# Loads of x in an FFT-mixing and feed-forward kernel: eight single steps or four pairs

## The chip, the cores and the metric

The kernel runs on one core of one Trainium2 chip. Its time is the device time of one execution in microseconds (us). Times of the kernel before are the median of three runs; a profile is one further execution with the hardware profiler.

## The reference

Eight sequences of 3008 positions by 256 channels are filtered in the frequency domain along the positions, and the result goes through a feed-forward layer with a PReLU-like step:

```python
X = np.fft.rfft(x, axis=1)                      # x: (8, 3008, 256)
Y = X * (filt_r + 1j * filt_i)[None, :, :]
y = np.fft.irfft(Y, n=3008, axis=1)             # then (24064, 256)
h = y @ w_in                                    # (256, 2048)
g = np.maximum(h, 0.0) + alpha * np.minimum(h, 0.0)
out = g @ w_out                                 # (2048, 256)
```

Everything that is multiplied is in 16-bit floating point; inputs and the output in HBM are 32-bit.

## The kernel before

**Two works in one stream.** The feed-forward layer is cut into 48 blocks of 512 (sometimes 384) rows of y. Each block has 16 steps `j`, so there are 768 steps, and the main loop at the end of the kernel (from line 690) runs over them. In a step it issues, in this order: what was held back (`flush`), the `sums` of a block that are due, whatever `plan` holds for the step, the held-back additions (`settle`), the two matmuls of `up(j)` (line 498), and then so many matmuls of an earlier block's second product as keep that about 17 steps behind (`LAG`).

**The FFT of the next batches is threaded through this by a plan written by hand.** `put(step, fn, ...)` appends a call to a step's list; calls of one step run in the order in which they were put. A batch covers six blocks, so its period is 96 steps, and for batch `b` the plan counts from `p = 96 * (b - 1)`. The stages of a batch are

- `load_x` (line 170): x of the batch goes from HBM to the tile `xs`, cast to 16 bits. A batch has four chunks `c` (0 to 3), each with two halves `h` of 47 partitions; one half is one transfer of 188 KB, issued on GpSimd's queue (POOL). `xs` has four buffers.
- `piece_a` (line 211): one matmul on `xs`; ScalarE evicts it to `asb`. Sixteen pieces, four for each chunk. `save_a` and `turn_a` move the result through HBM into `at`, on SyncE's queue (SP).
- `piece_b` (line 231): two matmuls on `at`; VectorE makes `ww` and `uu` (lines 234, 235), and two accumulating transfers on POOL's queue add `ww` into `uu` with halves swapped (line 237).
- `piece_c` (line 249): two matmuls on `uu`. `turn_c` (line 258) stores the result and `load_z` (line 267) loads it back as `zt`, both on SP's queue.
- `piece_d` (line 274): matmuls on `zt` that give `yT`, which the blocks read.

**Fast blocks.** Every second block from block 8 on (`FAST`) does its second product with seven half-size products in place of eight (`seven`, line 559). For that, sums of pieces of `gtb` are made beforehand (`sums`): some on VectorE, and some as accumulating transfers on POOL's queue (line 524), `gtb<-gtb` and, last, `gtb<-ss`. The last of the seven products reads what `gtb<-ss` wrote. In steps of a batch's period, the transfers of line 524 are due at steps 10, 17 and 20 of each pair of blocks, so at -22, -15, -12, 10, 17 and 20 around a period's start.

**The lines around the change.** `STEPS_Q` (line 39) holds the steps, counted from `p` of batch `b`, at which the eight halves of x of batch `b + 1` are loaded, for `b` of 3 to 6, that is, for batches four to seven; chunk `c`, half `h` uses entry `2 * c + h`:

```python
for h in range(2):
    put(p + STEPS_Q[2 * c + h], load_x, b + 1, c, (h,))
```

These are put ahead of the same batch's `piece_b`, so at an equal step the load comes first. The first `piece_a` of batch `b + 1` stands at step 12 of that count (`STEPS_A[0]` is -84 of the next period), those of the later chunks begin at steps 31, 40 and 46. The `piece_b` of batch `b` stand at `STEPS_B` (-21, -15, 4, 6, 13, 21, ...), and for `b = 3` at -11, -9, 0, 5, 10, 18, ...; `piece_c` of the third and fourth of them at 16 and 19 (`b = 3`: 16 and 22).

An engine's instructions run in the order in which they are issued, each waiting for what it needs; POOL's and SP's queues do so too.

Of the kernel before, what the change touches and what calls it, by code (L numbers as in the profile page):

```python
# [35 lines left out]
STEPS_F = (20, 16, 22, 28, 34)  # L36
STEPS_K = (118, 121, 128, 133, 144)
STEPS_X = ((20, 27, 42, 52), (107, 109, 113, 126))
STEPS_Q = (-28, -18, -8, -3, 1, 9, 15, 23)
FIRST = (  # L40
# [61 lines left out]
def kernel(  # L102
# [514 lines left out]
    def put(step, fn, *args):  # L617
        plan.setdefault(step, []).append((fn, args))
# [17 lines left out]
    for b in range(1, NB):  # L636
# [7 lines left out]
        if b + 1 < NB:  # L644
            for c in range(4):
                if b < 3:
                    put(STEPS_X[b - 1][c], load_x, b + 1, c)
                else:
                    for h in range(2):
                        put(p + STEPS_Q[2 * c + h], load_x, b + 1, c, (h,))  # L650
        quarters, later = (4, 1) if b < 3 else (1, 4)
# [97 lines left out]
```

## Time and profile before

| | us |
|---|---|
| median of 3 runs | 778.01 (777.71 to 780.72) |
| the profiled execution | 778.49 |
| its span | 776.7 |
| TensorE (PE) busy | 759.6 (98%) |
| VectorE (DVE) busy | 691.0 (89%) |
| ScalarE (ACT) busy | 606.1 (78%) |
| GpSimd (POOL) busy | 264.7 (34%) |

The granted TensorE clock was 0.997 over the span. "PEld" in the rows is the load of weights, which overlaps PE. A row of the timeline gives start, duration, engine, line, operation, tiles out<-in, how many were merged, and in brackets the idle time ahead with what ended it. A row of waits gives who waited for whom: total us, how often, longest. A row of windows gives the stretch, its length, each engine's busy time with its count, the PE clock, the share of the 16 DMA engines' time that was in use (overlaps can take it above 1) and GB/s. "DMA to landing" is the time from the start of an issue to the landing of its data.

### The profile page before, as it was taken

How to read it: one execution, taken by the hardware profiler on the slowest of the kernel's cores; microseconds unless marked ns; L12 is line 12 of the kernel's file. 1: busy time of each engine (PE TensorE's matmuls, PEld its weight loads, DVE VectorE, ACT ScalarE, POOL GpSimd, SP SyncE). 2: the span in 40 equal slices, each digit the busy share in tenths (PEclk: the TensorE clock that was granted, in tenths of full speed). 3: DMA queues.
4: the chain of work that ended last, by engine and by line, in shares of the span. 5: the costliest groups of instructions: out<-in, count | busy, mean ns of one | idle time of the engine just before them, and what ended most of it. 6: DMA issues, size and time to landing. Idle time of an engine off the chain costs nothing.

```text
span 776.7 us, 18287 instructions
## 1 busy us (share of the span) xinstructions
PE 759.6 (98%) x6952; PEld 541.9 (70%) x6952; DVE 691.0 (89%) x1517; ACT 606.1 (78%) x902; POOL 264.7 (34%) x351
## 2 busy tenths in 40 slices
PE   7899999999999999999999999999999999999998
PEld 6756667666676767766677767767677777777776
DVE  3788996799999999999899999989999999989994
ACT  4687678888788887888878888788878777787773
POOL 6830641144234342353233422434222333103210
PEclk9999999999999999999999999999999999999999
DMA  9996858666997679886797869966786645635642
GB/s 181 191 191 185 163 110 209 185 130 138 192 201 153 125 162 189 207 151 129 162 196 151 156 136 178 210 134 131 161 191 153 127 86 103 167 84 105 129 96 68
DMA packets 112879, 118.74 MB, mean 153 GB/s; under 512 B 12616, under 2 KB 94296, under 8 KB 112792
## 3 DMA queue, kind: packets, MB, share of 16 engines
q0 software_dynamic: 32656, 47.99, 38.4%
q1 hardware_dynamic: 79992, 69.52, 33.7%
q8 instruction: 54, 0.88, 0.5%
q14 instruction: 33, 0.27, 0.1%
q10 hardware_dynamic: 144, 0.07, 0.0%
HBM read 56.06 MB, written 46.66 MB: 132 GB/s over the span
## 4 chain that ended last, share of the span: by engine, by line
PE 87%; DVE 4%; DMA 4%; ACT 3%; issue 1%; POOL 1%; SPq 1%; DVEq 0%; ACTq 0%; POOLq 0%
PE hps L498 38%; PE op L537 20%; PE op L559 16%; PE psF L211 3%; PE psF L274 3%; PE psF L249 2%; PE psF L231 2%; ACT gtb L506 2%; DMA twf_s<-c_twf 1%; DVE m L509 1%; DVE gtb L685 1%; DMA zt<-v_dram 1%; PE op L592 1%; DVE ww L234 1%; DVE uu L235 1%
## 5 line engine op out<-in xcount | busy, mean ns | idle before, releaser
L506 ACT ACTIVATE gtb<-hps 128x1024 f16<-128x1024 f32 (+1 forms) x384 | 385.9, 1005 | 110.5 <-PE hps L498 106.5
L498 PE MATMUL hps<-yT,win_s 128*128 128x512 f16 (+1 forms) x1536 | 449.2, 374 | 0.0
L509 DVE TENSOR_SCALAR m<-gtb,alm_s 128x512 f16<-128x512 f16 (+1 forms) x768 | 235.1, 348 | 45.4 <-ACT gtb L506 43.7
L685 DVE TENSOR_TENSOR gtb<-gtb,m 128x1024 f16<-128x1024 f16 (+1 forms) x384 | 260.9, 679 | 14.2
L537 PE MATMUL op<-wout_s,gtb 128*128 128x256 f16 x1600 | 243.1, 272 | 0.0
L237 POOL DMA_DIRECT2D uu<-ww x168 | 142.2, 1014 | 263.1 <-DVE uu L235 165.2
L537 PEld LDWEIGHTS <-gtb 128*128 128x128 f16 x1600 | 156.0, 98 | 104.6
L498 PEld LDWEIGHTS <-win_s 128*128 128x128 f16 x1536 | 136.7, 98 | 25.6 <-issue 2.5
L559 PEld LDWEIGHTS <-gtb 128*128 128x128 f16 x1680 | 114.3, 98 | 53.8 <-DMA gtb<-ss 1.0
L524 POOL DMA_DIRECT2D gtb<-gtb x42 | 40.5, 963 | 192.9 <-DVE ss L518 62.1
L559 PE MATMUL op<-wout_s,gtb 128*128 128x128 f16 x1008 | 85.1, 219 | 1.1 <-ACT gtb L506 0.6
L281 ACT ACTIVATE asb<-psF 96x512 f16<-96x512 f32 x112 | 65.1, 594 | 9.7 <-PE psF L211 8.4
L281 ACT ACTIVATE yT<-psF 128x376 f16<-128x376 f32 x120 | 56.2, 486 | 10.5 <-PE psF L274 9.3
L559 PEld LDWEIGHTS <-ss 128*128 128x128 f16 x672 | 47.1, 98 | 23.3
L170 POOL DMA_DIRECT2D xs<-in_x_dram x64 | 54.4, 1014 | 14.2 <-PE psF L211 13.4
L559 PE MATMUL op<-tw_s,gtb 128*128 128x128 f16 x672 | 58.1, 219 | 0.0
L559 PE MATMUL op<-tw_s,ss 128*128 128x128 f16 x672 | 58.0, 219 | 0.0
L234 DVE TENSOR_TENSOR ww<-psF,filts_s 128x512 f16<-128x512 f32 x84 | 57.4, 684 | 0.3 <-PE psF L231 0.2
L235 DVE TENSOR_TENSOR uu<-psF,filt_s 128x512 f16<-128x512 f32 x84 | 57.2, 681 | 0.0
L281 ACT ACTIVATE v<-psF 128x512 f16<-128x512 f32 x84 | 49.0, 598 | 7.8 <-PE psF L249 7.2
L211 PE MATMUL psF<-xs,wf_s 94*96 94x512 f16 x112 | 41.2, 380 | 1.4 <-ACT yT L281 0.4
L274 PE MATMUL psF<-wi_s,zt 96*128 96x94 f16 x504 | 39.4, 205 | 2.2 <-ACT yT L281 1.4
(86 smaller groups left out, 524.9 us busy)
## 6 DMA issues: line engine op xcount, KB each, us to landing
out_dram<-osb SPq DMA_DIRECT2D x127, 128.0 KB
xs<-in_x_dram POOLq DMA_DIRECT2D x64, 188.0 KB, 5.8
a_dram<-asb SPq DMA_DIRECT2D x28, 384.0 KB
uu<-ww POOLq DMA_DIRECT2D x168, 64.0 KB, 3.0
v_dram<-v SPq DMA_DIRECT2D x112, 96.0 KB
zt<-v_dram SPq DMA_DIRECT2D x28, 384.0 KB
gtb<-gtb POOLq DMA_DIRECT2D x42, 256.0 KB, 4.5
at<-a_dram SPq DMA_DIRECT2D x20, 384.0 KB
```

The source lines that it names most:

```text
L211: nc.tensor.matmul(ps[0:96], wf1_s, xs[:, o : o + 512], start=True, stop=True)
L234: nc.vector.tensor_mul(ww, px, filts_s[:, 2 * kp : 2 * kp + 2])
L235: nc.vector.tensor_mul(uu, px, filt_s[:, 2 * kp : 2 * kp + 2])
L237: nc.gpsimd.dma_start(out=uu[o : o + 64], in_=ww[64 - o : 128 - o], accum_op=OP.add)
L274: nc.tensor.matmul(ps[:, m], self.zt[g][:, 4 * mh + m, dh * 128 : dh * 128 + 128], wi3_s, start=True, stop=True)
L281: nc.scalar.activation(o, i, AF.Copy)
L498: nc.tensor.matmul(self.hps[:, j % 2, 0:tn], win_s[:, kt, j * 128 : (j + 1) * 128], yT[:, kt, self.t0 : self.t0 + tn], start=(kt == 0), st ...
L506: nc.scalar.activation(g, hs, AF.Copy)
L509: nc.vector.tensor_scalar(ms[:, i], g[:, i], 0.0, a, OP.min, OP.mult)
L537: nc.tensor.matmul(op[:, si % 2], self.pair(k // 2)[:, k % 2, 128 * si : 128 * si + 128], wout_s[:, k], start=(k == 0), stop=(k == 15))
L559: nc.tensor.matmul(acc[:, 128 * i : 128 * i + 128], x[:, k, 128 * i : 128 * i + 128], b[:, k], start=first and k + i == 0, stop=k == 7, sk ...
L685: nc.vector.tensor_add(g, g, ms)
```

## The change

The eight steps of `STEPS_Q` become four equal pairs. Chunk 0 is loaded at -8 (both halves), chunk 1 at -4, chunk 2 at 0, chunk 3 at 4. Batches one to three are loaded as before.

```diff
-STEPS_Q = (-28, -18, -8, -3, 1, 9, 15, 23)
+STEPS_Q = (-8, -8, -4, -4, 0, 0, 4, 4)
```

## Prediction

> **What bounds the kernel now.** I read the page first: busy shares, the chain that ended last, the queues.
>
> ```profile
> span 776.7 us, 18287 instructions
> PE 759.6 (98%) x6952; PEld 541.9 (70%) x6952; DVE 691.0 (89%) x1517; ACT 606.1 (78%) x902; POOL 264.7 (34%) x351
> PE 87%; DVE 4%; DMA 4%; ACT 3%; issue 1%; POOL 1%; SPq 1%; DVEq 0%; ACTq 0%; POOLq 0%
> q0 software_dynamic: 32656, 47.99, 38.4%
> ```
>
> TensorE (PE) is busy for 98% of the span and is 87% of the chain. q0 holds the transfers that GpSimd (POOL) issues, the loads of x among them. The next view is busy time by windows, one window of 91 us for about each period of 96 steps in which the moved loads lie (us, then PE, PEld, DVE, ACT, POOL busy with counts, PE clock, DMA share, GB/s).
>
> ```profile
> 200.00:291.00 91.00, 90.72 (x825) 63.78 (x824) 84.31 (x185) 74.50 (x111) 33.66 (x42) 1.00 0.80 164
> 291.00:382.00 91.00, 90.15 (x839) 64.02 (x837) 85.33 (x191) 74.64 (x113) 32.87 (x43) 1.00 0.79 164
> 382.00:473.00 91.00, 91.00 (x831) 64.17 (x830) 84.75 (x186) 74.93 (x113) 31.14 (x41) 1.00 0.79 164
> 473.00:564.00 91.00, 90.09 (x835) 63.94 (x834) 84.89 (x191) 74.51 (x114) 32.94 (x43) 1.00 0.78 164
> ```
>
> PE's idle time in the four periods is 0.28 + 0.85 + 0.00 + 0.91 = 2.04 us. The change adds and removes no matmul, so 2.04 us is about all it can win; what it can lose has no such bound. So the question is which late transfer makes PE wait, and I asked for the waits in the last of the four periods and for the chain there.
>
> ```profile
> PE psF L274 <- DMA zt<-v_dram: 0.3, 1, 0.3
> PEld L559 <- DMA gtb<-ss: 0.8, 1, 0.8
> ```
> ```profile
> 490.32 3.22 DMA v_dram<-v
> 493.68 6.09 DMA zt<-v_dram
> ```
> ```profile
> 499.81 0.51 PE L274 MATMUL psF<-wi_s,zt 96*128 96x94 f16 x8 [0.28 <-DMA zt<-v_dram]
> 506.70 0.28 PE L559 MATMUL op<-wout_s,gtb 128*128 128x128 f16 x2 [0.62 <-ACT gtb L506]
> ```
>
> Two transfers arrive just too late: the first zt tile (0.28 us of idle PE) and gtb<-ss, the accumulate that the last product of a fast block reads (the weight load waited 0.8 us for it, PE idled 0.62 us; the matmul row names ACT, but the weight load in front of it names the DMA). 0.28 + 0.62 is that period's 0.91.
>
> **What the change moves.** POOL's timeline for that period (p = 480, the loads of batch seven):
>
> ```profile
> 475.12 1.21 POOL L170 DMA_DIRECT2D xs<-in_x_dram  x1
> 491.10 1.65 POOL L237 DMA_DIRECT2D uu<-ww  x2 [1.32 <-DVE uu L235]
> 492.16 1.14 POOL L170 DMA_DIRECT2D xs<-in_x_dram  x1
> 496.53 0.97 POOL L524 DMA_DIRECT2D gtb<-gtb  x1 [3.23 <-PE op L559]
> 500.01 1.51 POOL L524 DMA_DIRECT2D gtb<-ss  x1
> 500.59 2.54 POOL L170 DMA_DIRECT2D xs<-in_x_dram  x3
> 513.42 1.74 POOL L237 DMA_DIRECT2D uu<-ww  x2 [10.28 <-DVE uu L235]
> 515.74 1.74 POOL L237 DMA_DIRECT2D uu<-ww  x2 [0.58 <-DVE uu L235]
> 516.93 1.10 POOL L170 DMA_DIRECT2D xs<-in_x_dram  x1
> ```
>
> POOL works its list in order and does not follow PE's steps: it runs ahead until something makes it wait. The loads of steps -8, -3 and 1 already go out together at 500.59, right behind gtb<-ss (step -12), because nothing stands between them. All eight steps of the new list lie between that gtb<-ss and the uu of step 4 (the loads of step 4 are planned ahead of that uu). So the eight will go out as one burst from 500.59, not as four pairs; 475.12 (-28), 492.16 (-18), 516.93 (9) and the two after it (15, 23) go. In the period of batch three the uu steps are other (-11, -9, 0, 5), so there six go out, then a uu, then two.
>
> **Cost on POOL.** Nothing is added: the same eight issues. POOL idled 10.28 us before 513.42. Three issues began within one row of 2.54 us, so eight need at most 8 x 1.2 = 9.6 us (the longest single issue above is 1.21) and end by 510.2, ahead of 513.42. If that cover were gone, each extra microsecond would hold up the uu.
>
> There is one wait that the burst may bring: POOL waits for its own old transfers when many are out. At the start, where it issues loads in a row, it shows
>
> ```profile
> POOL filt_s L178 <- DMA xs<-in_x_dram: 1.6, 3, 0.7
> ```
>
> filt_s has nothing to do with xs, so these are waits for a free slot; the queue's semaphores come round. I take it that eight can be out. Then the loads behind the fourth wait until gtb<-gtb (496.53), the uu and gtb<-ss have landed, and the last load goes out when gtb<-ss lands, about 506.7. What queues behind it is the uu of 513.42, which by then needs only the first loads to have landed. Cost 0 while that is before 513.42.
>
> **Cost on the DMA engines.** Here is the real price.
>
> ```profile
> DMA to landing us min/median/max: 8.1/8.6/8.7
> DMA to landing us min/median/max: 4.0/4.0/4.0
> DMA to landing us min/median/max: 2.4/2.7/3.3
> ```
> ```profile
> 500.00:505.00 5.00, 5.00 (x76) 4.20 (x74) 4.67 (x14) 4.71 (x10) 3.13 (x5) 1.00 1.13 252
> 505.00:510.00 5.00, 4.38 (x50) 3.11 (x48) 3.25 (x9) 3.69 (x8) 0.00 (x0) 1.00 0.92 212
> 510.00:515.00 5.00, 4.99 (x40) 3.36 (x39) 4.94 (x11) 3.79 (x6) 1.58 (x2) 1.00 0.33 87
> 515.00:520.00 5.00, 5.00 (x39) 3.34 (x37) 4.86 (x12) 4.54 (x8) 3.33 (x5) 1.00 0.61 80
> 520.00:525.00 5.00, 5.00 (x41) 3.32 (x40) 4.93 (x11) 4.65 (x8) 2.22 (x3) 1.00 0.82 167
> ```
>
> The first three rows are times from issue to landing: the three loads sent together, the lone load of 516.93, the six uu from 513.42 on. How long does one load occupy the engines? From q0's row, 0.384 x 776.7 us for 47.99 MB is 6.2 us per MB; a load of 188 KB (0.193 MB) is then 1.2 us. The bounds: 0.193 MB at the 252 GB/s of the first window, 0.76 us; and the lone load's 4.0 us. The upper one can't be a rate, since three loads sent within about 1 us landed within 0.6 us of each other, so I take 1.2 us.
>
> The burst has five loads more than the three: 6.0 us of work. The engines are full until about 510 and idle for 5 x 0.67 + 5 x 0.39 = 5.3 us between 510 and 520, and the lone load that leaves that stretch frees 1.2. So the burst is through at about 510 + 6.0 + what the SP queue moves there (about 5 x 0.33 = 1.7) = 517.7. The uu of 513.42 stands behind it in q0 and lands at about 517.7 + 1 = 518.7 in place of 513.42 + 2.7 = 516.1. Who waits for it:
>
> ```profile
> 517.78 0.38 PE L211 MATMUL psF<-xs,wf_s 94*96 94x512 f16 x1
> 521.56 0.38 PE L249 MATMUL psF<-uu,twi_s 128*128 128x256 f16 x2
> 524.29 0.38 PE L249 MATMUL psF<-uu,twi_s 128*128 128x256 f16 x2
> ```
>
> L249 reads this uu at 521.56 and the next one (515.74, by then landing near 520) at 524.29: 2.9 and 4 us to spare. The first pair of loads lands as today's first two did, by 500.59 + 0.6 + 8.6 = 509.8, 8 us before L211 reads it at 517.78; the later pairs have longer. Cost 0 in each case, with a cover of 2.9 us as the thinnest.
>
> The Trainium skill's page "DMA: Bandwidth & Descriptors", section "Rules for kernel authors", speaks against the change: issue a transfer early and wait for it late. The first pair is issued later here, by 25.5 us in this trace. The rule's damage would be a wait at L211, which is a rival below; the trace so far shows 8 us of cover against it.
>
> **What it wins.** The load at 492.16 was out just before the zt loads of 493.68 and the gtb<-gtb of 496.53; with its 1.2 us gone, zt and the accumulates behind it can land up to 1.2 us sooner. This covers the 0.28 and the 0.62 (0.8 at the weight load). What is late next is the work itself: PE never idles otherwise there. In 291:382 the same two places lie within the 0.85, of which I count a quarter, since half of its waits name no transfer. Sum: -0.28 - 0.62 - 0.2 + 0 = about -1.0 us; bounds -2.0 (all idle time) and, if the moved load does not reach those transfers, 0. The profiled execution took 778.49 us, 0.48 above the median of 778.01 of the runs; so 777.5 for its like, 777.0 for the median.
>
> **Rivals.** (a) *The burst slows the gtb<-ss in front of it.* Issue to landing of gtb<-ss at step -12 in the periods from 291, 382, 473 and 564 us; the first three have three loads behind it, the last has none:
>
> ```profile
> gtb<-ss POOLq DMA_DIRECT2D x1, 256.0 KB, 7.1
> gtb<-ss POOLq DMA_DIRECT2D x1, 256.0 KB, 8.6
> gtb<-ss POOLq DMA_DIRECT2D x1, 256.0 KB, 6.6
> gtb<-ss POOLq DMA_DIRECT2D x1, 256.0 KB, 5.6
> ```
>
> That is 1.0 to 3.0 us more with three loads, 0.3 to 1.0 per load. Were it the loads' doing, five more would make it 1.7 to 5.0 us later, and this accumulate has no cover (0.8 us of wait already). In three periods that is 5 to 15 us, less the 1.0: 782 to 792, with 783 to 786 the likelier end because at most one more load goes out before the older transfers land. It decides from 1.3 us per period on. Against it: zt on the SP queue is moving at the same time, which alone can explain the spread, and the loads are queued behind, not ahead. The same page of the Trainium skill, section "Queues, rings and completion order", says that an engine takes a ring's descriptors in their order; by that the loads behind would cost nothing. 22%.
>
> (b) *The uu of steps 4 and 6 come late.* If a load takes 2.0 us and not 1.2, the burst ends 8 x 0.8 = 6.4 us later than worked out, the uu is 3.5 us late at L249, and four periods cost up to 14 us: 784 to 791. It decides from 1.6 us per load on. Against it: the 0.6 us between the landings of three loads. 5%.
>
> (c) *The first pair is late at L211*: needs 8 us more; 1.5 us beyond that in four periods is 6 us, 783. 2%.
>
> (d) *More won than PE's idle time shows*, since its busy time is modelled: over 3.9 us, about 773.5. Only 2.04 us of idle time speaks for it. 4%.
>
> (e) *Nothing moves*: the early loads did not delay zt, and the burst is hidden: 778.0. It differs from the forecast by less than can be measured; both together have 67%.
>
> **The numbers.** 777.0 is the forecast. 0.5% is 3.9 us, about what a measurement of this kernel can tell from no change. Forecast and (e) lie within it, 67%, and so does the mild end of (a), 1%: same 0.68. Slower: 21 + 5 + 2 = 0.28. Faster: (d), 0.04. The range goes from 775.5 (the 2.0 us bound and some spread of the runs) to 783.0, the low end of (a), which leaves out (d) and the upper parts of (a) and (b).
>
> **What would show it.** Right: in POOL's timeline one row of eight xs (or four and four) right behind gtb<-ss at step -12, no xs between zt and it; DMA share near 1.0 in 510 to 517; the uu after it landing 2 to 3 us later than now, and no PE wait at L249; no more waits of L274 for zt and of L559 for gtb<-ss. Wrong: gtb<-ss landing over 8 us after its issue in every period with L559 waiting for it (a), waits of L249 for uu (b), of L211 for xs (c), or PE idle of over 1 us in a period for a cause not named here.

## The result and the profile after

| | before, us | changed, us |
|---|---|---|
| median | 779.33 (777.71 to 783.6, 19 runs) | 776.65 (775.82 to 778.02, 19 runs) |
| profiled execution, its span | 778.49, 776.7 | 777.9, 776.1 |

The ratio is 0.9968, with a 95% interval of 0.9958 to 0.9978: about 2.5 us (1.7 to 3.3) less. That is inside the range given and inside 0.5%, on the side that was forecast, and two and a half times as much as was forecast. In these runs the spread fell too: 5.9 us from lowest to highest before, 2.2 us changed.

The page of the changed kernel: busy time and the issuing queue are as they were.

```profile
span 776.1 us, 18294 instructions
PE 757.3 (98%) x6952; PEld 539.8 (70%) x6952; DVE 690.6 (89%) x1517; ACT 605.7 (78%) x902; POOL 264.0 (34%) x351
q0 software_dynamic: 32656, 47.99, 38.0%
```

The windows of the four periods, as in the prediction:

```profile
200.00:291.00 91.00, 90.72 (x826) 63.80 (x825) 84.27 (x185) 74.48 (x111) 33.31 (x42) 1.00 0.77 164
291.00:382.00 91.00, 90.18 (x840) 64.11 (x838) 85.56 (x192) 74.87 (x113) 33.14 (x43) 1.00 0.78 164
382.00:473.00 91.00, 91.00 (x833) 64.17 (x832) 84.76 (x186) 74.98 (x113) 30.99 (x40) 1.00 0.77 163
473.00:564.00 91.00, 90.99 (x851) 64.92 (x850) 86.06 (x193) 74.99 (x115) 34.05 (x44) 1.00 0.78 166
```

PE's idle time in the last of them went from 0.91 to 0.01 us; the other three did not move (0.28, 0.82, 0.00). So in this pair of executions the change shows in one place, the last product of block 28, which reads the gtb<-ss of step -12 (step 468 of 768, 20 steps into the pair of blocks that begins with block 28). POOL's timeline there:

```profile
496.23 0.98 POOL L524 DMA_DIRECT2D gtb<-gtb  x1 [3.77 <-PE op L559]
497.20 1.70 POOL L237 DMA_DIRECT2D uu<-ww  x2
499.58 0.95 POOL L524 DMA_DIRECT2D gtb<-ss  x1 [0.68 <-PE psF L274]
500.16 4.11 POOL L170 DMA_DIRECT2D xs<-in_x_dram  x7
505.41 0.51 POOL L170 DMA_DIRECT2D xs<-in_x_dram  x1 [1.14 <-DMA gtb<-ss]
511.89 1.74 POOL L237 DMA_DIRECT2D uu<-ww  x2 [5.97 <-DVE uu L235]
```

The four pairs are one burst right behind gtb<-ss, and the eighth load waited 1.14 us until gtb<-ss had landed, a transfer that it has nothing to do with: the free slot of the prediction. It delayed nobody, since POOL was idle again for 5.97 us before the uu.

Time from issue to landing: first gtb<-ss at step -12 in the periods from 291, 382, 473 and 564 us (the last has no loads behind it), then the first two loads of the burst, then the two uu from 511.89 on.

```profile
gtb<-ss POOLq DMA_DIRECT2D x1, 256.0 KB, 5.1
gtb<-ss POOLq DMA_DIRECT2D x1, 256.0 KB, 5.0
gtb<-ss POOLq DMA_DIRECT2D x1, 256.0 KB, 5.5
gtb<-ss POOLq DMA_DIRECT2D x1, 256.0 KB, 5.2
```
```profile
DMA to landing us min/median/max: 5.8/6.8/7.9
DMA to landing us min/median/max: 4.7/4.8/5.0
```

With eight loads behind it gtb<-ss lands in 5.0 to 5.5 us, where with three behind and one ahead of it it took 6.6 to 8.6. The cover is still thin: the one of the period from 473 us lands at 499.58 + 5.5 = 505.1 and is first read at 505.18 (first row of the second fence below). In the second profile of the changed kernel it lands at 498.82 + 4.1 = 502.9 and is read at 504.43. The DMA engines are full until about 515 (517.7 was worked out), and PE's reads find their data:

```profile
505.00:510.00 5.00, 5.00 (x53) 3.65 (x51) 4.18 (x10) 4.40 (x8) 0.51 (x1) 1.00 1.03 217
510.00:515.00 5.00, 4.99 (x41) 3.30 (x39) 5.00 (x12) 3.64 (x6) 2.53 (x4) 1.00 1.02 231
515.00:520.00 5.00, 5.00 (x34) 3.21 (x33) 4.86 (x11) 4.50 (x8) 1.84 (x3) 1.00 0.67 115
```
```profile
505.18 0.28 PE L559 MATMUL op<-wout_s,gtb 128*128 128x128 f16 x2
516.26 0.38 PE L211 MATMUL psF<-xs,wf_s 94*96 94x512 f16 x1
520.03 0.38 PE L249 MATMUL psF<-uu,twi_s 128*128 128x256 f16 x2
```

### The profile page after: what moved, and what is told of

It reads as the page before. It is cut to its first block, busy times and chain, and to the rows that moved or that the text cites. A ratio compares the mean times of both kernels' runs of the same rounds, so it can differ in the third digit from the quotient of the medians.

```text
span 776.1 us, 18294 instructions
## 1 busy us (share of the span) xinstructions
PE 757.3 (98%) x6952; PEld 539.8 (70%) x6952; DVE 690.6 (89%) x1517; ACT 605.7 (78%) x902; POOL 264.0 (34%) x351
## 4 chain that ended last, share of the span: by engine, by line
PE 89%; DVE 4%; DMA 3%; ACT 2%; issue 1%; POOL 0%; DVEq 0%; ACTq 0%; POOLq 0%
PE hps L498 39%; PE op L537 20%; PE op L559 17%; PE psF L211 3%; PE psF L274 3%; PE psF L249 2%; PE psF L231 2%; ACT gtb L506 1%; DVE m L509 1%; DMA xs<-in_x_dram 1%; DVE gtb L685 1%; DMA twf_s<-c_twf 1%; PE op L592 1%; DMA uu<-ww 1%; DVE ww L234 1%
## 5 line engine op out<-in xcount | busy, mean ns | idle before, releaser
L170 POOL DMA_DIRECT2D xs<-in_x_dram x64 | 40.9, 915 | 16.9 <-PE psF L211 14.1
```

## The experiments

Theory A: the gain comes from the two early loads (-28, -18) leaving their place in front of the zt loads and of the accumulates at -15 and -12, which have no cover. Theory B: it comes from the three late loads (9, 15, 23). Theory C: half from each.

**The two kernels again.** No edit, and the whole edit.

> The kernel before, once more, as the yardstick and for a second profile of it. Every theory: ratio 1.000. Theory A (the loads of steps -28 and -18 stand in front of the zt loads and of the accumulate gtb<-ss of step -12, which have no cover): the waits of L274 for zt and of L559 for gtb<-ss appear again in the periods from 291, 382 and 473 us, in other sizes than in the first profile (0.3 and 0.8 us there), since the runs of this kernel spread over 6 us and those of the changed one over 2 us. Theory B (the loads of steps 9, 15 and 23 run into the accumulates and uu of steps 10 to 25): the waits that come and go are those of L249 for uu or of L559 after step 20.

> The changed kernel, once more. Every theory: ratio 0.997 (776.6 against 779.3), no wait of PE for zt or gtb<-ss over 0.1 us in the four periods.

The unchanged kernel gave 0.9997 (0.9984 to 1.001), the changed one 0.9976 (0.9963 to 0.9989). The smaller spread did not come back: 777.33 to 781.32 us in 12 runs of the unchanged kernel, 775.05 to 779.67 in 12 of the changed one. The waits of PE in the last period, and the windows around block 28, of the unchanged kernel's second profile, an execution of 781.32 us:

```profile
PE op L559 <- DMA gtb<-ss: 2.6, 1, 2.6
```
```profile
500.00:505.00 5.00, 5.00 (x76) 4.20 (x74) 4.83 (x16) 4.91 (x11) 2.77 (x5) 1.00 1.13 265
505.00:510.00 5.00, 2.39 (x19) 1.42 (x17) 2.01 (x5) 1.16 (x3) 0.00 (x0) 0.85 0.93 180
510.00:515.00 5.00, 4.99 (x41) 3.57 (x40) 2.78 (x7) 3.61 (x6) 0.00 (x0) 0.81 0.19 51
```

The same wait as in the first profile, but 2.6 us and not 0.6, and behind it the granted clock averages 0.85 and 0.81 over two windows of 5 us. In windows of 1 us it is 0.50 from about 508.5 to 511.9 us, for 3.4 us, and 1.00 before and after; one of them:

```profile
509.00:510.00 1.00, 1.00 (x7) 0.44 (x5) 0.00 (x0) 0.00 (x0) 0.00 (x0) 0.50 0.36 91
```

The second profile of the changed kernel has no wait for a transfer in the four periods. PE's wait for zt was not there in this execution of the unchanged kernel, and neither was a wait for gtb<-ss in the periods from 291 and 382 us, where the expectation had them too.

**The same again, twice, for the profile alone.**

> The kernel before, one more profile. If the wait of L559 for block 28's gtb<-ss is what differs from execution to execution: again another size, between 0.5 and 4 us, and the granted clock in the 10 us behind it is 1.00 if the wait is under 2 us and under 0.9 if it is over 2.5 us. If the wait is fixed: 0.6 to 0.8 us as in the first profile.

> The kernel before, a third further profile, with the same expectation: a wait of L559 at block 28 of another size than 0.6 and 2.6 us if it differs from execution to execution, of 0.6 to 0.8 us if it is fixed.

```profile
PE op L559 <- DMA gtb<-ss: 1.5, 1, 1.5
505.00:510.00 5.00, 4.14 (x43) 3.08 (x44) 3.02 (x8) 2.77 (x6) 0.00 (x0) 1.00 0.88 225
```
```profile
PE op L559 <- DMA gtb<-ss: 2.1, 1, 2.1
505.00:510.00 5.00, 2.85 (x27) 1.95 (x25) 1.95 (x5) 1.81 (x4) 0.00 (x0) 0.84 0.98 222
510.00:515.00 5.00, 4.99 (x38) 3.17 (x36) 3.29 (x8) 3.41 (x7) 0.00 (x0) 0.82 0.31 95
```

The first fence is the wait and window of the run labelled unchanged2 (777.78 us), the other those of unchanged3 (780.79 us), which also waits 0.4 us for a gtb<-ss in the period from 200 us. So the wait differs from execution to execution: 0.6, 2.6, 1.5 and 2.1 us in four profiles of one program, taking 778.49, 781.32, 777.78 and 780.79 us. The two over 2 us are followed by a lower clock, and theirs are the two long times. That 778.49 lies above 777.78, although the wait was shorter, has another place behind it: the first profile has a granted clock of 0.50 from about 21.7 to 25.1 us, at the start of the kernel. The lost clock is 5 x 0.16 + 5 x 0.18 = 1.7 us of TensorE work in the last of the four, on top of the wait. The expectation put the point between 2 and 2.5 us open; 2.1 us was enough.

PE's busy time is modelled, so it helps to time this place by another engine. ScalarE evicts at line 506 384 times in every execution. From the start of the 233rd of these to that of the 249th it takes 29.2, 32.4, 29.8 and 31.9 us in the four profiles of the unchanged kernel, and 28.0 us in both profiles of the changed one. From the 249th to the last it takes 241.9 us in all six. So this place alone costs the unchanged kernel 1.2 to 4.4 us more.

**Early loads alone, late loads alone.**

```diff
-STEPS_Q = (-28, -18, -8, -3, 1, 9, 15, 23)
+STEPS_Q = (-8, -8, -8, -3, 1, 9, 15, 23)      # early
+STEPS_Q = (-28, -18, -8, -3, 1, 4, 4, 4)      # late
```

> Only the loads of steps -28 and -18 are moved, to -8; those of 9, 15 and 23 stay. Theory A: the whole gain, ratio 0.997, zt and gtb<-ss land with 1 to 4 us more cover. Theory B: ratio 1.000. Theory C (the gain comes from having few transfers in flight after step 4, half from each end): 0.9985.

> Only the loads of steps 9, 15 and 23 are moved, to 4; those of -28 and -18 stay. Theory A: ratio 1.000, the waits for zt and gtb<-ss stay as before. Theory B: ratio 0.997. Theory C: 0.9985.

Early: 0.9968 (0.9955 to 0.998), the whole gain. Late: 1.0005 (0.9991 to 1.0018), nothing. By the times theory A holds and B falls; C's 0.9985 lies outside both intervals. One thing does not fit A as put: the profile of the early kernel still has the wait (first row), as the late one has (second row).

```profile
PE op L559 <- DMA gtb<-ss: 1.1, 1, 1.1
```
```profile
PE op L559 <- DMA gtb<-ss: 1.7, 1, 1.7
```

The 1.1 us of the early kernel lie within the 0.6 to 2.6 us of the unchanged one, and from the 233rd to the 249th eviction it takes 29.2 us (the late kernel 29.8). So this profile does not show what the early loads' leaving does to the wait; that it gives the gain is shown by the times alone. Both stayed at a clock of 1.00 there. How often the wait is over 2 us in each kernel can't be had from one profile.

**The -18 load alone.**

```diff
-STEPS_Q = (-28, -18, -8, -3, 1, 9, 15, 23)
+STEPS_Q = (-28, -8, -8, -3, 1, 9, 15, 23)
```

> Of the old steps only -18 is moved, to -8; -28, 9, 15 and 23 stay. If it is the load out just before the zt loads that delays them and the accumulates behind: the whole gain, 0.997. If the load of -28, which moves beside the turn of the A stage 15 us before, takes a part: 0.998 to 0.999. If neither: 1.000.

0.9978 (0.9961 to 0.9995), with a wait of 0.8 us for gtb<-ss in its profile. That excludes "neither" and does not tell "all" from "most": whether the load at -28 has a share stays open.

**One period alone.**

```diff
-put(p + STEPS_Q[2 * c + h], load_x, b + 1, c, (h,))
+put(p + (STEPS_Q if b < 6 else (-8, -8, -4, -4, 0, 0, 4, 4))[2 * c + h], load_x, b + 1, c, (h,))
```

> The new steps for batch seven alone (the period from 473 us); batches four to six are loaded at the old steps. Theory A1 (one place: block 28's gtb<-ss, whose landing PE awaited for 0.8, 2.6 and 1.7 us in three profiles with the old steps): the whole gain, ratio 0.997, and no wait of L559 for gtb<-ss at about 505 us. Theory A2 (each of the four periods wins a share): 0.9992. Nothing in this period: 1.000.

0.9971 (0.9955 to 0.9987), and PE waits for no transfer in that period; from the 233rd to the 249th eviction it takes 28.0 us. One of the four periods gives the gain, within what the interval can tell; A2's 0.9992 lies outside.

From issue to landing, block 28's gtb<-ss took 6.6, 8.2, 7.3 and 7.7 us in the four profiles of the unchanged kernel, 7.2 in the late one, 6.8 in the early one and 6.4 with -18 alone moved, but 5.5 and 4.1 in the two of the changed kernel and 4.1 in this one. So the transfer lands clearly sooner with the new steps; that the two early loads by themselves bring it there, one profile of each does not show, and why it was still at 6.8 us with both of them out of the way stays open.

**Old steps, without the transfer that PE waits for.** In `sums`, kind 4 is the addition by a transfer (line 524) and kind 6 the same addition on VectorE (line 526).

```diff
-ahead.setdefault(16 * n + at, []).append((blk, w, h))
+ahead.setdefault(16 * n + at, []).append((blk, 6 if (n, w) == (28, 4) else w, h))
```

> All loads at the old steps; in block 28 alone the sum that the transfer gtb<-ss makes is made by VectorE (one more tensor_add of 0.68 us there, one transfer less). Theory A1: the gain without moving a load, ratio 0.997 to 0.9975 (the 0.3 us for zt stays), PE no longer waits at block 28's last product. Theory A2: 0.9992 or, as VectorE is 89% busy, up to 1.001.

0.9975 (0.9959 to 0.9991): with no load moved, taking this one accumulate from the DMA queue to VectorE gives a gain of this size too, and the place takes 28.2 us. Its profile also shows that the old steps leave other places open: two waits for gtb<-ss and one for gtb<-gtb in the periods from 200 and 291 us, 1.7 us together.

```profile
PE op L559 <- DMA gtb<-ss: 1.0, 2, 0.7
PE op L559 <- DMA gtb<-gtb: 0.7, 1, 0.7
```

**Both edits**, the new steps and block 28's sum on VectorE.

> The changed kernel, and block 28's gtb<-ss made by VectorE as before. If that transfer still makes PE wait in some executions with the new steps (its cover was 0.05 and 1.5 us in two profiles): 0.996. If the new steps have taken all of it: as the changed kernel, 0.997, or 0.1% above it for the VectorE work.

0.9964 (0.9948 to 0.998), a median of 776.65: not to be told from the changed kernel's 0.9968. The interval holds the 0.996 of the other expectation as well, so the ratio does not decide between them; but from the 233rd to the 249th eviction its profile takes 28.0 us, as both of the changed kernel do. In these executions the new steps have taken what there was at that place.

**All eight in front.**

```diff
-STEPS_Q = (-28, -18, -8, -3, 1, 9, 15, 23)
+STEPS_Q = (-18, -18, -18, -18, -18, -18, -18, -18)
```

> All eight loads at -18, in front of the zt loads and of the accumulates of steps -15 and -12. Theory A with q0 in order and both queues sharing the engines: eight loads are 9.6 us of engine time ahead of both, zt lands 4 to 8 us later against a cover of 0 to 2.5 us and gtb<-ss 4 to 8 us later against 0 to 1: 4 to 7 us in each of four periods, 795 to 807 (ratio 1.02 to 1.036). If the place of the loads does not matter to what is behind them: 0.997 to 1.000.

1.0371 (1.0344 to 1.0398), 809.49 us: by the ratio 29 us more, just above the top of the expected. PE's waits in the four periods (200 to 565 us), and POOL in the period from 382 us:

```profile
PE op L559 <- DMA gtb<-gtb: 13.4, 3, 5.4
PE psF L274 <- DMA zt<-v_dram: 8.9, 1, 8.9
PE op L559 <- DMA gtb<-ss: 0.7, 1, 0.7
```
```profile
417.35 3.72 POOL L170 DMA_DIRECT2D xs<-in_x_dram  x6
423.16 1.01 POOL L170 DMA_DIRECT2D xs<-in_x_dram  x2 [2.09 <-DMA uu<-ww]
425.16 0.93 POOL L524 DMA_DIRECT2D gtb<-gtb  x1 [0.99 <-DVE m L509]
```

23 us of waits. Two things hold up the gtb<-gtb: its transfer goes behind eight loads, and POOL itself stood 2.09 us at the seventh load, until an older uu had landed, before it could issue it. So a burst of the same size, 10 to 22 steps earlier, costs 29 us where the changed kernel's wins 2.5. The granted clock goes with it (10 us that hold most of the wait of 8.9 us):

```profile
230.00:240.00 10.00, 3.56 (x24) 2.44 (x25) 1.57 (x5) 2.16 (x4) 0.00 (x0) 0.59 0.59 156
```

**All eight behind the uu of step 4.**

```diff
-STEPS_Q = (-28, -18, -8, -3, 1, 9, 15, 23)
+STEPS_Q = (5, 5, 5, 5, 5, 5, 5, 5)
```

> All eight loads at step 5, behind the uu of step 4 and ahead of that of step 6 (for batch four: at the uu of step 5 of batch three). Nothing of x stands in front of zt or of gtb<-ss any more, nor behind them within 10 us. Rival (a) of the prediction: gtb<-ss at step -12 lands sooner than with the burst behind it, by 1 us or more. No such effect: the same 4.2 to 5.6 us. The first pair goes out at about 515.5 in the last period and lands 8.3 us later, 523.8, against the read at 516.3: about 7 us of waiting at L211 in each of four periods, and the uu of step 6 is late as well: 800 to 810 (ratio 1.027 to 1.04). If the loads are faster than worked out, as a lone one's 4.0 us: 3 us per period, 1.015.

1.0125 (1.0106 to 1.0144), 789.67 us: slower, but by 10 us, not 20 to 30. PE's waits in the four periods, and gtb<-ss of step -12 in the periods from 291, 382 and 473 us, now with nothing behind it:

```profile
PE psF L211 <- DMA xs<-in_x_dram: 5.2, 4, 1.9
PE psF L249 <- DMA uu<-ww: 4.6, 3, 1.9
```
```profile
gtb<-ss POOLq DMA_DIRECT2D x1, 256.0 KB, 4.4
gtb<-ss POOLq DMA_DIRECT2D x1, 256.0 KB, 5.3
gtb<-ss POOLq DMA_DIRECT2D x1, 256.0 KB, 4.3
```

Both waits are where they were expected, but the loads came sooner:

```profile
DMA to landing us min/median/max: 4.5/6.9/9.2
```

The first of the eight took 4.5 us, near the lone load's 4.0, where 8.3 had been taken over from loads that stood behind accumulates. And gtb<-ss without the burst behind it lands in 4.3 to 5.3 us, against 5.1, 5.0 and 5.5 us in the changed kernel's profile and 4.9, 5.0 and 4.1 us in its second one. The means are 4.7, 5.2 and 4.7 us; in a single period the largest difference is 5.5 - 4.3 = 1.2 us. So the burst costs it half a microsecond or less on average, where rival (a) priced it at 1.7 to 5.0.

## Why the prediction was right, and where it was short

**Order on POOL: right.** One burst behind gtb<-ss at step -12, no load between zt and it, and no harm from the wait for a slot. It had the wait begin behind the fourth load; seven were out before the visible one, which ended when gtb<-ss landed, as told. In the period of batch three, six loads, a uu and two loads went out, as told (POOL from 228.19 us in the changed kernel's profile).

**DMA price: right.** The cover of the uu of step 4 was to be 2.9 us. Issued at 511.89 and half a microsecond later, landing 4.7 to 5.0 us on, it is there at about 517.2 and read at 520.03: 2.8 us. The first pair was to have 8 us; it lands by 500.16 + 0.6 + 7.9 = 508.7 and is read at 516.26: 7.6 us. The eight loads landed from 506.0 to 515.3 us, 1.3 us apart (an estimate from these two landings), where 1.2 was taken. One reading behind the 1.2 was wrong: the 0.6 us are the difference of three times from issue to landing. The loads were issued over 1.06 us and landed over about 1.6 us, 0.8 us apart, which also lies below 1.2, so the sum did not suffer by it.

**What goes: right in kind.** The early loads were named as what delays the two transfers without cover, and the times of the early kernel and of the one with -18 alone bear it out. The place was narrower than told: of zt's 0.28 us of idle PE less than 0.1 us came again in any of the three further profiles of the unchanged kernel, and the new steps in the period of block 28 alone gave the gain, as far as the interval can tell. The quarter of the 0.85 us counted in the period from 291 did not come (0.85 became 0.82), though the VectorE run shows that this period can lose time in other executions.

**What was mis-sized: the sum's term for gtb<-ss, and the bound.** The 0.62 us was read from one execution, and "2.04 us is about all it can win" was the idle time of that one. Three further profiles of the same kernel had 2.6, 1.5 and 2.1 us at that spot, 2.62 us of idle in this window alone for the first of them (91.00 - 88.38):

```profile
473.00:564.00 91.00, 88.38 (x805) 62.87 (x803) 81.63 (x184) 72.04 (x111) 31.57 (x40) 0.98 0.75 156
```

The mean over the four is 1.7 us in place of 0.62. Nor had the sum a term for the clock that a long wait can cost, 1.7 us in two of these four. Two of four is not the share in the runs, though. One such drop gives a granted clock of 0.998 over the span (1.7 of 777 us). Of the runs of the unchanged kernel taken with the experiments 26 of 92 are at 0.998 or less, of those of the changed kernel 5 of 31 (19 and 12), and some of these drops lie elsewhere, as the first profile's at 22 us. Among the runs at 1.00 the medians are 778.68 us (54 runs) and 776.46 us (20 runs), still 2.2 us apart. So most of the gain comes without a lost clock. The two profiles of the unchanged kernel without one at this place cost 1.2 and 1.9 us there; what makes up the rest of the 2.5 us is not shown.

That the number fell inside the range is in part luck: the forecast of -1.0 us rested on a single execution's wait, and the gain went past the 2.04 us that was called all it can win.

**The rivals.** (a) fell: half a microsecond or less on average. (b) did not come about, with 2.8 us left. (c) is real in kind, as the run with all loads at step 5 shows, but has 7.6 us of cover here. (d) had it that more can be won than PE's idle time shows; that is so here, not for the reason given but because the idle time was that of one execution, and 2.5 us is short of its 3.9. (e) fell: the interval leaves out 1.000. The Trainium skill's rule (page "DMA: Bandwidth & Descriptors", section "Rules for kernel authors"), to issue early, would have kept the loads at -28 and -18. The measurement decides against it here: later by 20 and 10 steps was 0.3% faster, since the loads had cover to spare and the transfers behind them had none. At step 5 the cover is gone and the rule holds.

## What to carry to other kernels

Rank transfers by their cover, landing to first read, and not by how early they can go: one with 20 us of cover must not stand ahead of one with none in the same queue or on the same engines, and a burst right behind the urgent one cost it half a microsecond or less on average. Before taking a wait's size from a profile, look at it in a second and third execution: a wait with hardly any cover was 0.6 to 2.6 us in four of them, and it is priced by its mean. A queue that is issued in order carries its old transfers with it: here, with eight out, the issuing engine itself stood still until an old one had landed.

## What the runs showed of the hardware that was not expected

PE's waits of 2.6 and 2.1 us for gtb<-ss were each followed, 0.6 and 1.0 us after their end, by a granted clock of 0.50 for about 3.4 us, which is 1.7 us of TensorE work lost. After the waits of 0.6, 0.8, 1.1, 1.5 and 1.7 us it stayed at 1.00. With all loads at step 5, a wait of 1.91 us was followed by the same drop (from about 345.2 to 348.5 us) and one of 1.93 us was not:

```profile
344.07 0.38 PE L249 MATMUL psF<-uu,twi_s 128*128 128x256 f16 x2 [1.91 <-DMA uu<-ww]
526.45 0.39 PE L211 MATMUL psF<-xs,wf_s 94*96 94x512 f16 x1 [1.93 <-DMA xs<-in_x_dram]
```

In the wait of 8.9 us with all loads at -18 the clock went to 0.50 some 4.4 us into the wait. The Trainium skill, page "TensorE: Matmul & The Clock Gate", section "Part 1: The HAM clock gate (the "warmup" mystery)", puts the step down after at least one idle window of about 3.4 us; here reported waits of 2.6, 2.1 and 1.9 us were enough, so that figure is too long as a safe limit for this kernel. By the two waits of 1.9 us the length of the wait alone does not decide; what else does, the runs do not show.

With gtb<-ss and seven loads out, eight transfers, POOL waited for gtb<-ss to land before it issued the eighth load: 1.14 us in the changed kernel. With all loads at -18 it was 2.09 us, for a uu, with two uu and six loads out. In both traces POOL's transfers use eight semaphores in turn (numbers 99 to 106), and each issue waits for its own, so the eight are those of this program; whether the queue itself could hold more is not shown.
